# Casting loads head by head for v and the tails of batches 0 to 2, and another order of the first three tiles, in a fused attention and ReGLU kernel

## The chip, the cores and the metric

The kernel runs on one core of one Trainium2 chip. A core has a matrix engine (TensorE, PE in the profile; its weight loads are listed apart as PEld), a vector engine (VectorE, DVE), a scalar engine (ScalarE, ACT), GpSimd (POOL) and a synchronising engine (SyncE, SP), which here only issues DMAs. The on-chip memories are SBUF and PSUM; PSUM has eight banks, and PE writes only there. The metric is the device time of one launch in microseconds (us); the kernel's time is the median over its runs.

## The reference

Eight batches of eight heads, 576 positions, 64 values a head, in f32. Attention is causal by blocks of 64: a position sees its own block and all before it. The result, 4608 tokens of 512 values, goes through a ReGLU feed-forward of width 1536.

```python
scores = scale * np.matmul(q, k.transpose(0, 1, 3, 2))
scores = np.where(block_i >= block_j, scores, -1e9)
attn = exp(scores - max); attn = attn / (sum + 1e-9)
x = matmul(attn, v) laid out as 4608 x 512
out = (maximum(x @ w_gate, 0) * (x @ w_val)) @ w_out
```

## The kernel before

**Tiles.** The kernel computes in bf16 with f32 sums. The feed-forward runs over nine tiles of 512 tokens: tiles 0 to 7 hold the first 512 positions ("mains") of batches 0 to 7, tile 8 the last 64 positions ("tails") of all batches. Tile j needs the attention of batch j, transposed to `xT`. So attention of batch j+1 is woven into the feed-forward of tile j, and tile 0 stands behind a head that does the attention of batch 0 with no feed-forward beside it.

**Places.** A generator `ffn_gen` emits the feed-forward product by product. Everything else is an *act*, a named piece of work, with a *place* in the table `AT`: the number of products that come before it. A tile has 144 places in `AT`: 96 of gate and value products (L1095), 48 of output products (L1199 in tiles 0 and 1; from tile 2 on the output products are 42 pairs, L793, and the places are scaled). Tile 1 begins at place 144, tile 2 at 288, tile 3 at 432. Acts are emitted in the order of their places, and the order in which each engine works is the order of emission. An engine thus stands at an instruction whose input is late, and all that is emitted behind it on this engine waits. SP and POOL run ahead of PE's places as far as data and buffers allow. A product's result on PE goes to one of three PSUM banks `ffnp`, is relued by ACT (L1105, gate) and multiplied by DVE (L1115, value) into `hT`; the bank is then free.

**Acts of a round.** A round r is one pair of heads of batch r // 4. `s` computes its scores (PE, L454) and the first exps (ACT), `e` the last exp, `c` zeroes the masked corners, `a` and `b` multiply by v for the two heads (PE, L589) and normalise (DVE, into `xnat`), and `x` transposes into `xT`: rounds 4 to 7 on PE, from round 8 on by a DMA transpose from SP's queue (L638). Tails of batches 0 to 2 have acts of their own: `S`, `E`, `L` (scores, exps, last keys), `A` and `B` (products with v). From batch 3 on the tails are part of the rounds.

**Getting q, k and v in.** For batches 0 to 2, SP loads f32 into buffers `stage` (ten of 128 x 1024, in rotation), and an engine casts to bf16:

- q and k (`E1q0`, `E1q4`, `E1q6`, `E2q0`, `E2q4`): each partition gets four neighbouring positions of a head, 1 KB in one piece. Casts: `q0`, `k0`, `q4`, `q6`, and inside `q2`, `q24`.
- v: batch 1 head by head (L162, acts `E1v0`, `E1v4`, casts `ev0`, `ev4` on POOL, L223), batch 2 by chunks of 128 positions (`E2v0`, `E2v4`, L172, casts in `v2` on POOL, L231). Pieces of 256 B.
- tails of q, k and v (`T0`, `T1`, `T2`, L184), cast by `tc` on POOL (L209, L210, L217) and `td` on DVE.

The mains of batch 1 are then transposed on PE, one pair of heads at a time (`m0` to `m3`, L272, evicted by ACT and DVE, L281). Those of batch 2 are transposed by DMA into `perm` (L245, from `q2` and `q24`), and `u0` to `u3` bring them into order (L256).

From batch 3 on, POOL issues *casting loads* (L341): DMAs that read f32 from HBM and write bf16 to SBUF, with pieces of 256 B read and 128 B written. `l3` loads q and k of batch 3, `lv3` its v, `l4` and `lv4` those of batch 4. They need no stage and no cast. `dq3`, `d3`, `d4` are the DMA transposes behind them on SP (L350). `behind` in `load_qkv` is an instruction that the first load of a group waits for; `products[-1]` is the last gated product of DVE that has been emitted.

Weights come through `stage` too: `cg..`, `cv..`, `cw..` are the casts of pieces of the gate, value and output weights (L386); `w00` to `w21` load the output weights. `W0` to `W5` are sums of output weights on POOL (L698, L699). `o0` to `o3` store tile 0's output. `HOW` gives the engine of each act.

Of the kernel before, what the change touches and what calls it, by code (L numbers as in the profile page):

```python
# [11 lines left out]
BF = mybir.dt.bfloat16  # L12
# [5 lines left out]
def kernel(  # L18
# [10 lines left out]
    nc = tc.nc  # L29
# [94 lines left out]
    class Early:  # L124
# [33 lines left out]

        def load_v(self, h0, n):
# [127 lines left out]

        def pe_tails(self, evac):
# [14 lines left out]
    products = []  # L303
# [785 lines left out]
    def ffn_gen():  # L1089
        for j in range(B + 1):  # L1090
# [3 lines left out]
            def product(to, t, c, f):  # L1094
                nc.tensor.matmul(  # L1095
# [5 lines left out]
                )  # L1101

# [95 lines left out]
            def out_mm(op, s, f, n0, n1):  # L1198
                nc.tensor.matmul(  # L1199
# [5 lines left out]
                )  # L1205

# [61 lines left out]
    with tc.manual_schedule(engines={E.PE, E.DVE, E.Activation, E.Pool, E.SP}):  # L1268

        e0, e1, e2 = [Early(b) for b in range(3)]  # L1270
        w = {}
# [46 lines left out]
        def v_2():  # L1318
            e2.cast_v_chunks(0, pool)
            e2.cast_v_chunks(1, pool)  # L1320

# [3 lines left out]
        def mains_2(h0):  # L1325
            e2.cast_qk(h0, 4, (pool, pool))
            e2.transpose(h0 // 4)

        def load_tails(e):
            e.load_tails((0, 1))  # L1330
            e.load_tails((2,))
# [18 lines left out]

        def mains_1(hp):
            engs, banks = HOW[f"m{hp}"]
            if banks == "one":
                both = bank("one", BF)
                two = [both[:, 512 * t : 512 * t + 512] for t in range(2)]
            else:
                two = [bank(w, BF)[:, 0:512] for w in banks]
            e1.pe_mains(hp, [by[e] for e in engs], two)
# [88 lines left out]
            "E1v0": 32.16,  # L1447
# [3 lines left out]
            "E1v4": 32.19,  # L1451
            "T0": 32.19,
            "E2q0": 32.19,
            "T1": 32.23,
# [9 lines left out]
            "ev0": 32.33,  # L1464
# [3 lines left out]
            "ev4": 34.05,  # L1468
            "tc0": 34.05,
            "q2": 37.71,  # L1470
            "tc1": 48.64,
# [5 lines left out]
            "E2v0": 109.09,  # L1477
# [9 lines left out]
            "E2v4": 125.35,  # L1487
            "T2": 126.26,
# [17 lines left out]
            "td0": 156.81,  # L1506
            "t0": 163.43,
            "td1": 164.5,
# [10 lines left out]
            "v2": 191.07,  # L1519
# [10 lines left out]
            "tc2": 214.11,  # L1530
            "td2": 214.72,
# [66 lines left out]
            "m0": (("act", "dve"), "one"),  # L1598
            "m1": (("dve", "act"), ("sc", "ffn")),
            "m2": (("act", "act"), ("sc", "ffn")),  # L1600
            "m3": (("act", "act"), "one"),
# [41 lines left out]
        }  # L1643
        STEADY = {"s": 2, "e": 8, "c": 15, "a": 22, "b": 26, "x": 26.1}
# [49 lines left out]
            "E1q0": lambda: e1.load_qk(0, 4),  # L1694
            "E1q4": lambda: e1.load_qk(4, 2),
            "E1q6": lambda: e1.load_qk(6, 2),
            "E1v0": lambda: e1.load_v(0, 4),
            "E1v4": lambda: e1.load_v(4, 4),
            "T0": lambda: load_tails(e0),
            "T1": lambda: load_tails(e1),  # L1700
            "T2": lambda: load_tails(e2),
            "E2q0": lambda: e2.load_qk(0, 4),
            "E2q4": lambda: e2.load_qk(4, 4),
            "E2v0": lambda: e2.load_v_chunks(0),
            "E2v4": lambda: e2.load_v_chunks(1),
            "q0": lambda: e1.cast_qk(0, 4, (pool, None)),
            "k0": lambda: e1.cast_qk(0, 4, (None, by[HOW["k0"]])),
            "q4": lambda: e1.cast_qk(4, 2, [by[e] for e in HOW["q4"]]),
            "q6": lambda: e1.cast_qk(6, 2, [by[e] for e in HOW["q6"]]),
            "ev0": lambda: e1.cast_v(0, 4, pool),  # L1710
            "ev4": lambda: e1.cast_v(4, 4, pool),
            **{f"tc{b}": lambda e=e: e.cast_tails(True, 0, pool) for b, e in enumerate((e0, e1, e2))},
            **{f"td{b}": lambda e=e: e.cast_tails(False, 1, dve) for b, e in enumerate((e0, e1, e2))},
            **{f"m{hp}": lambda hp=hp: mains_1(hp) for hp in range(4)},
            "q2": lambda: mains_2(0),
            "q24": lambda: mains_2(4),
# [4 lines left out]
            "v2": v_2,  # L1721
# [7 lines left out]
            "lv4": lambda: load_qkv(4, (2,)),  # L1729
# [31 lines left out]
        for c in range(6):  # L1761
# [5 lines left out]
                "q2": 39.35,  # L1767
                "E2q4": 45.78,
                "s4": 94.33,
                "e4": 116.37,  # L1770
                "c4": 118.9,
                "e5": 119.89,
                "a4": 122.44,
                "b4": 122.71,
                "m2": 124.37,
                "c5": 124.58,
                "E2v4": 125.26,
                "a5": 126.96,
                "s6": 128.29,
                "b5": 128.47,  # L1780
                "e6": 128.55,
                "c6": 131.71,
                "x5": 133.24,
                "m3": 134.04,
                "x4": 137.38,
                "s7": 140.84,
                "b6": 140.91,
                "a6": 141.21,
                "e7": 142.62,
                "T2": 142.71,  # L1790
                "x6": 146.04,
                "c7": 147.83,
                "a7": 148.88,
                "b7": 149.16,
# [138 lines left out]
```

## Time and profile before

| what | value |
|---|---|
| time, median of 3 runs | 355.68 us (354.7, 355.68, 359.37) |
| the profiled execution's own time | 359.0 us |
| its span, first to last instruction | 357.1 us |
| mean granted clock of TensorE | 0.992 |
| PE / DVE / ACT / POOL busy | 96% / 60% / 55% / 47% |
| DMA | 155496 packets, 50.04 MB, 140 GB/s on average |
| the chain that ended last, by engine | PE 87%, DMA 4%, ACT 3%, DVE 3%, issue 1% |

The span is what the views of the trace divide up; the time of the launch lies some 1.9 us above it. A row of a timeline gives the start in us from the span's beginning, the length, the engine, the line of the kernel and the operation, with the tile that is written left of the arrow and those that are read right of it; in brackets stands how long the engine was idle before it, and who ended that. A row of a group gives the count, the busy time, the mean in ns of one, and after the bar the idle time in front of them. SPq and POOLq are the queues that issue DMAs. In a table by stage the busy times of the engines stand one after the other.

### The profile page before, as it was taken

How to read it: one execution, taken by the hardware profiler on the slowest of the kernel's cores; microseconds unless marked ns; L12 is line 12 of the kernel's file. 1: busy time of each engine (PE TensorE's matmuls, PEld its weight loads, DVE VectorE, ACT ScalarE, POOL GpSimd, SP SyncE). 2: the span in 40 equal slices, each digit the busy share in tenths (PEclk: the TensorE clock that was granted, in tenths of full speed). 3: DMA queues.
4: the chain of work that ended last, by engine and by line, in shares of the span. 5: the costliest groups of instructions: out<-in, count | busy, mean ns of one | idle time of the engine just before them, and what ended most of it. 6: DMA issues, size and time to landing. Idle time of an engine off the chain costs nothing.

```text
span 357.1 us, 8396 instructions
## 1 busy us (share of the span) xinstructions
PE 341.5 (96%) x3276; PEld 217.2 (61%) x3317; DVE 214.9 (60%) x552; ACT 196.8 (55%) x319; POOL 167.6 (47%) x199
## 2 busy tenths in 40 slices
PE   7889999999979999999999999999999999999994
PEld 3544455555534458555775567555855588888883
DVE  4654455667517566366636664567446657786783
ACT  4932756578322874555556553666266636735731
POOL 4647556579912930194009506980292042620630
PEclk9999999999998999999999999999999999999998
DMA  8999989999991999499739993999511013003005
GB/s 245 292 356 375 319 202 221 244 157 179 183 187 35 136 171 143 144 123 123 141 110 125 128 164 110 94 138 140 128 61 29 17 24 118 2 3 117 2 1 119
DMA packets 155496, 50.04 MB, mean 140 GB/s; under 512 B 134464, under 2 KB 151872, under 8 KB 155456
## 3 DMA queue, kind: packets, MB, share of 16 engines
q0 software_dynamic: 70480, 8.85, 47.5%
q1 hardware_dynamic: 79040, 33.96, 45.1%
q10 hardware_dynamic: 5936, 6.69, 5.8%
q8 instruction: 26, 0.43, 0.6%
q14 instruction: 14, 0.11, 0.1%
HBM read 37.75 MB, written 9.44 MB: 132 GB/s over the span
## 4 chain that ended last, share of the span: by engine, by line
PE 87%; DMA 4%; ACT 3%; DVE 3%; issue 1%; SPq 0%; POOL 0%; POOLq 0%; DVEq 0%
PE ffnp L1095 38%; PE ffnp L793 12%; PE upa L965 6%; PE one L793 5%; PE ffnp L1199 4%; PE sc L454 3%; PE upc L965 3%; PE ffnp L589 2%; DMA stage<-in_moe_w_gate_dram 2%; PE one L454 2%; DMA xT<-xnat 2%; ACT attnT L418 2%; PE ffnp L965 1%; PE one L589 1%; PE one L1095 1%
## 5 line engine op out<-in xcount | busy, mean ns | idle before, releaser
L1115 DVE TENSOR_TENSOR hT<-gate_sb,ffnp 128x512 bf16<-128x512 bf16 x82 | 56.1, 684 | 66.7 <-PE ffnp L1095 35.5
L1095 PE MATMUL ffnp<-xT,wg 128*128 128x512 bf16 x300 | 85.5, 383 | 4.4 <-DMA xT<-xnat 2.3
L1095 PE MATMUL ffnp<-xT,wv 128*128 128x512 bf16 x311 | 88.1, 382 | 1.4 <-issue 0.8
L1105 ACT ACTIVATE gate_sb<-ffnp 128x512 bf16<-128x512 f32 x79 | 48.0, 610 | 49.9 <-PE ffnp L1095 48.1
L459 ACT ACTIVATE attnT<-sc 128x1024 bf16<-128x1024 f32 x56 | 57.9, 1046 | 0.0
L1095 PEld LDWEIGHTS <-wg 128*128 128x128 bf16 x336 | 30.9, 98 | 36.5 <-issue 7.0
L1095 PEld LDWEIGHTS <-wv 128*128 128x128 bf16 x336 | 30.4, 98 | 33.8 <-issue 4.2
L341 POOL DMA_DIRECT2D q_bf<-in_q_dram x20 | 18.0, 913 | 53.2 <-DVE hT L1115 37.9
L825 ACT COPY ob<-ffnp 128x512 f32<-128x512 f32 x21 | 12.3, 585 | 43.7 <-PE ffnp L793 42.2
L793 PEld LDWEIGHTS <-stage 128*128 128x128 bf16 x336 | 32.5, 98 | 3.7
L589 PEld LDWEIGHTS <-attnT 128*128 128x128 bf16 x640 | 26.7, 98 | 12.6 <-issue 1.5
L793 PEld LDWEIGHTS <-hT 128*128 128x128 bf16 x252 | 24.1, 98 | 4.2 <-DVE hT L997 0.7
L341 POOL DMA_DIRECT2D v_bf<-in_v_dram x30 | 24.2, 857 | 1.5 <-DMA k_bf<-in_k_dram 0.9
L466 ACT ACTIVATE attnT<-one 128x512 bf16<-128x512 f32 (+1 forms) x28 | 15.1, 538 | 16.4 <-PE ffnp L454 15.5
L1199 PE MATMUL ffnp<-wo,hT 128*128 128x512 bf16 x89 | 22.2, 379 | 0.2
L454 PEld LDWEIGHTS <-kTm 64*128 64x128 bf16 x384 | 13.2, 94 | 14.2 <-issue 8.4
L793 PE MATMUL ffnp<-stage 128*128 128x256 bf16 x168 | 21.6, 273 | 0.0
L793 PE MATMUL ffnp<-wo,hT 128*128 128x256 bf16 x168 | 21.3, 273 | 0.1
L341 POOL DMA_DIRECT2D k_bf<-in_k_dram x20 | 18.0, 944 | 0.0
L454 PE MATMUL sc<-qTm,kTm 64*128 64x512 bf16 (+1 forms) x168 | 17.9, 305 | 0.0
L750 DVE TENSOR_TENSOR stage<-hT 128x512 bf16<-128x512 bf16 (+1 forms) x45 | 17.6, 394 | 0.5
L1001 POOL TENSOR_TENSOR hT<-attnT,gate_sb 128x512 bf16<-128x512 f32 x4 | 4.6, 1159 | 25.1 <-ACT gate_sb L1009 25.1
(185 smaller groups left out, 618.8 us busy)
## 6 DMA issues: line engine op xcount, KB each, us to landing
out_dram<-ob ACTq DMA_DIRECT2D x24, 256.0 KB, 2.3
stage<-in_moe_w_val_dram SPq DMA_DIRECT2D x6, 512.0 KB, 8.6
stage<-in_moe_w_gate_dram SPq DMA_DIRECT2D x6, 512.0 KB, 8.9
stage<-in_moe_w_out_dram SPq DMA_DIRECT2D x6, 512.0 KB, 10.5
q_bf<-in_q_dram POOLq DMA_DIRECT2D x20, 128.0 KB, 4.4
k_bf<-in_k_dram POOLq DMA_DIRECT2D x20, 128.0 KB, 6.0
v_bf<-in_v_dram POOLq DMA_DIRECT2D x20, 128.0 KB, 6.1
stage<-in_v_dram SPq DMA_DIRECT2D x19, 128.0 KB, 5.7
```

What stands on the lines that cost most here:

```text
L341: ins = nc.gpsimd.dma_start(dst, part_of)
L454: nc.tensor.matmul(o, kTm[b % 2][head_of(hh), c, hp, :], qT, start=True, stop=True)
L459: return lambda: nc.scalar.activation(at[:, :, lo : lo + 512], sc, AF.Exp, scale=scale)
L466: nc.scalar.activation(at[:, hh, 1024 : 1024 + w], third[hh][:, 0:w], AF.Exp, scale=scale)
L589: nc.tensor.matmul(av[:, p, :], at[:, col : col + 128], v_bf[b % 2][:, c, h, :], start=(p == 0), stop=(c == p), skip_group_check=True,)
L750: ins = (eng or nc.vector).tensor_tensor(out=s(i), in0=a, in1=b, op=op)
L793: nc.tensor.matmul(to, sums.of(c)[which]()[:, 128 * p : 128 * p + 128], right, start=first, stop=(c == 5), skip_group_check=True,)
L965: nc.tensor.matmul(to[:, 256 * f : 256 * f + 256], left(which, u // 2)[:, kc, lo : lo + 128], right[which](kc), start=new and (f, kc) == ( ...
L1095: nc.tensor.matmul(to, (wg, wv)[t][f // 4][:, c, 128 * (f % 4) : 128 * (f % 4) + 128], x[:, c], start=(c == 0), stop=(c == 3),)
L1105: nc.scalar.activation(gate_sb, gate, AF.Relu)
L1115: nc.vector.tensor_tensor(out=h, in0=gate_sb, in1=val, op=AX.mult)
L1199: nc.tensor.matmul(op, hT[f][:, 128 * s : 128 * (s + 1)], wo[f // 4][:, f % 4, n0:n1], start=(f == 0), stop=(f == 11),)
```

## The change

Five things change.

1. v of batches 1 and 2, and the tails of q, k and v of batches 0 to 2, are loaded by casting loads from POOL, two heads an act (`E1v0` to `E1v3`, `E2v0` to `E2v3`), with acts for the tails (`E1v4`, `E0v`, `E2v4` for v, `T0` to `T2` for q and k). The casts `ev0`, `ev4`, `v2`, `tc` and `td` are gone. The first load of each act waits for the last gated product that was emitted before it.
2. q and k of batch 1's second half are loaded four heads at a time (`load_wide`), and each is one cast instead of two. The loads wait for the last product of PE emitted before them (`marks`), except `E1q0`.
3. The transposes of batch 1 on PE are made for two pairs of heads at a time into two whole banks (`pe_wide` in `m0` and `m2`), and evicted pair by pair (`evac_wide`).
4. `l3`, `lv3` and `lv4` also wait for the last gated product.
5. The places of acts in tiles 0 to 2, and the engines of some casts and copies, are others.

```diff
+        def load_wide(self, hg, ts, tied=True):
+            behind = marks[-1] if tied and marks else None
+            for t in ts:
+                st = self.st[t, 4 * hg] = new_stage(1024)
+                ins = nc.sync.dma_start(
+                    st.rearrange("p (h n) -> p h n", h=4),
+                    (q, k)[t][self.b, 4 * hg : 4 * hg + 4, 0:512, :].rearrange(
+                        "h (p j) d -> p h (j d)", j=4
+                    ),
+                )
+                after(ins, behind)
+                behind = None
...
+        def casting_loads(self, pieces):
+            behind = products[-1] if products else None
+            for dst, src in pieces:
+                after(nc.gpsimd.dma_start(dst, src), behind)
+                behind = None
...
+        def load_v_casting(self, hp):
+            self.casting_loads(
+                [
+                    (
+                        v_bf[self.b % 2][:, 0:4, h, 0:64],
+                        v[self.b, h, 0:512, :].rearrange("(c p) d -> p c d", p=128),
+                    )
+                    for h in (2 * hp, 2 * hp + 1)
+                ]
+            )
...
+        def pe_wide(self, hg, two):
+            for t in range(2):
+                src = self.half(t, hg)
+                for i in range(8):
+                    nc.tensor.transpose(
+                        two[t][:, 128 * i : 128 * i + 128],
+                        src[:, i % 4, 128 * (i // 4) : 128 * (i // 4) + 128],
+                        ident,
+                    )
...
+                marks[:] = [ins]
...
+        def mains_2(hg):
+            for t in range(2):
+                e2.cast_wide(hg, t, pool)
+            e2.transpose(hg)
...
-            "l3": lambda: load_qkv(3, (0, 1)),
+            "l3": lambda: load_qkv(3, (0, 1), products[-1]),
...
-            "lv3": lambda: load_qkv(3, (2,)),
+            "lv3": lambda: load_qkv(3, (2,), products[-1]),
```

`load_v_tails` and `load_qk_tails` do the same for the last 64 positions: two loads for v, one for q and two for k, each of 512 pieces for q and 256 for the others.

The diff sets places in several layers; the net result for the acts that the text speaks of (a dash: there is no such act):

| act | place before | place after | act | place before | place after |
|---|---|---|---|---|---|
| `E1q0` | 20.29 | 31.89 | `u0` | 190.06 | 175.71 |
| `E1v0` | 32.16 | 32.25 | `E2v1` | - | 177.64 |
| `E2q4` | 45.78 | 32.32 | `u2` | 208.80 | 178.42 |
| `E1v1` | - | 32.65 | `E2v0` | 109.09 | 181.56 |
| `q4` | 32.36 | 33.06 | `E2v3` | - | 183.06 |
| `q6` | 32.36 | 44.94 | `u1` | 186.30 | 189.62 |
| `E1v2` | - | 81.55 | `E2v2` | - | 197.17 |
| `E1v3`, `E1v4` | -, 32.19 | 95.0 | `l3` | 218.57 | 206.37 |
| `T1` | 32.23 | 95.13 | `E2v4` | 125.26 | 233.2 |
| `e4` | 116.37 | 95.19 | `b10` | 257.52 | 254.65 |
| `T0` | 32.19 | 113.05 | `a11`, `b11` | 255.82, 255.91 | 256.06, 256.15 |
| `o0` | 211.88 | 121.41 | `x9` | 257.80 | 257.80 |
| `E0v` | - | 122.63 | `x10` | 258.51 | 265.03 |
| `m2`, `m3` | 124.37, 134.04 | 123.01, 126.7 | `x11` | 256.77 | 269.13 |
| `a5` | 126.96 | 129.46 | `lv3` | 267.98 | 299.67 |
| `E2q0` | 32.19 | 131.52 | `l4` | 319.56 | 319.14 |
| `q2`, `q24` | 39.35, 191.07 | 133.73, 137.09 | `a12` | 344.19 | 340.47 |
| `W0` | 224.67 | 165.0 | `d4` | 341.28 | 362.52 |
| `T2` | 142.71 | 169.39 | `x13` | 360.22 | 366.57 |

Engines: `cg00/01` and `cv00/23` go from DVE to ACT, `cg00/23` and `cv10` from POOL to ACT, `cv00/01` from DVE to POOL, `cv20` from POOL to DVE, `cw21/1` from DVE to ACT. The second half of `u0` goes from POOL to ACT, the first half of `u2` from DVE to ACT, the second half of `u1` from DVE to POOL.

More of the change, by code (lines that the diff above doesn't have):

```diff
@@ L1349, in piece @@
             return lambda: cast_w(w[n], by[HOW.get("c" + name, "pool")], rows)
+        wide = {}
         def mains_1(hp):
             engs, banks = HOW[f"m{hp}"]
[L1353 to L1358, printed above, removed]
+            hg = hp // 2
+            if hp % 2 == 0:
+                wide[hg] = [bank(n, BF) for n in banks]
+                e1.pe_wide(hg, wide[hg])
+            e1.evac_wide(hp, wide[hg], [by[n] for n in engs])
         AT = {
@@ L1446 @@
             "w10": 32.12,
-            "E1v0": 32.16,
+            "E1v0": 16.06,
+            "E1v1": 32.25,
+            "E1v2": 32.26,
+            "E1v3": 32.27,
             "w21": 32.16,
@@ L1486 @@
             "c5": 124.67,
-            "E2v4": 125.35,
-            "T2": 126.26,
+            "E2v4": 180,
+            "T2": 164,
             "a5": 127.05,
@@ L1885 @@
                 "e16": 440.19,
+                "L4": 440.2,
                 "c16": 446.75,
+            }
+        )
+        AT.update(
+            {
+                "E1q0": 7.94,
+                "E1v1": 30.9,
+                "w01": 31.9,
+                "w00": 32.05,
+                "E1v0": 32.28,
+                "E1v2": 32.29,
+                "E2q0": 32.29,
+                "E1v4": 32.32,
+                "q4": 33.06,
+                "q6": 39.6,
+                "cv20": 39.67,
+                "E0v": 59.28,
+                "q2": 83.63,
+                "m0": 83.76,
+                "e4": 114.3,
+                "T0": 116.1,
+                "c4": 119.55,
+                "b4": 122.07,
+                "c5": 122.64,
+                "a4": 122.93,
+                "m2": 123.01,
+                "m3": 126.7,
+                "a5": 129.46,
+                "b5": 130.09,
+                "s7": 136.5,
+                "c6": 137.1,
+                "a6": 140.99,
+                "x6": 149.0,
+                "x7": 152.75,
+                "T2": 167.67,
+                "E0": 168.68,
+                "A0": 176.07,
+                "E1": 194.84,
+                "t2": 215.84,
+                "E2v4": 233.82,
+            }
+        )
```

458 lines of the change are left out of this document (317 added, 141 removed).

## The prediction

> **What bounds the kernel now.** I read the page's engine totals first, then the 40 slices, then busy time by stage, then who made TensorE (PE) wait.
>
> ```profile
> span 357.1 us, 8396 instructions
> PE 341.5 (96%) x3276; PEld 217.2 (61%) x3317; DVE 214.9 (60%) x552; ACT 196.8 (55%) x319; POOL 167.6 (47%) x199
> ...
> PEclk9999999999998999999999999999999999999998
> GB/s 245 292 356 375 319 202 221 244 157 179 183 187 35 136 171 143 144 123 123 141 110 125 128 164 110 94 138 140 128 61 29 17 24 118 2 3 117 2 1 119
> q0 software_dynamic: 70480, 8.85, 47.5%
> ```
>
> PE is busy in 341.5 of 357.1 us and no other engine passes 60%. The change leaves PE's work as it is: 32 transposes of 128x128 for batch 1 stay 32, and no product is added or dropped. It can therefore only act through the 357.1 - 341.5 = 15.6 us in which PE stands still, and through its clock. The stages show where those lie (columns: window; length; busy time and count of PE, PEld, DVE, ACT, POOL; PE clock; DMA share; GB/s):
>
> ```profile
> 0.00:10.00 10.00, 7.32 (x42) 3.27 (x42) 4.50 (x14) 5.34 (x7) 4.88 (x20) 1.00 0.87 252
> 10.00:20.00 10.00, 8.45 (x131) 5.60 (x129) 7.70 (x23) 7.41 (x11) 5.22 (x11) 1.00 1.16 303
> 20.00:30.00 10.00, 9.04 (x45) 4.06 (x45) 4.12 (x9) 4.58 (x8) 5.82 (x6) 1.00 1.08 366
> 50.00:60.00 10.00, 9.84 (x113) 5.68 (x115) 5.40 (x19) 9.10 (x16) 4.62 (x7) 1.00 0.94 215
> 100.00:110.00 10.00, 7.69 (x38) 3.25 (x38) 2.56 (x5) 2.61 (x4) 0.00 (x0) 0.83 1.13 169
> 320.00:358.00 38.00, 32.26 (x291) 27.97 (x288) 24.93 (x47) 17.00 (x31) 10.21 (x9) 0.96 0.20 56
> ```
>
> The first 30 us lose 2.7 + 1.6 + 1.0 = 5.2 us while the first weights arrive, and the end loses 5. Between them one stage stands out, 100 to 110 us: 2.3 us idle, and a granted clock of 0.83, which is half speed for 3.4 us, another 1.7 us. Together **4.0 us are lost at the step from tile 1 to tile 2**. The timeline of PE and of SP's queue, then the chain that ended last, name the cause:
>
> ```profile
> 102.79 0.38 PE L1095 MATMUL ffnp<-xT,wg 128*128 128x512 bf16 x1
> 104.58 0.38 PE L1095 MATMUL ffnp<-xT,wg 128*128 128x512 bf16 x1 [1.29 <-DMA xT<-xnat]
> 105.92 1.01 PE L1095 MATMUL ffnp<-xT,wg 128*128 128x512 bf16 x2 [0.96 <-DMA xT<-xnat]
> ...
> 88.95 4.70 SPq L350 DMA_TRANSPOSE qTm<-q_bf  x1
> 96.00 4.65 SPq L638 DMA_TRANSPOSE xT<-xnat  x3
> ...
> 98.07 1.26 SPq L638
> ...
> 99.43 6.44 DMA xT<-xnat
> ...
> 92.96 4.83 POOL L341 DMA_DIRECT2D v_bf<-in_v_dram  x6
> ```
>
> Tile 2 needs four DMA transposes (`x8` to `x11`). Three were queued together at 96.00: `x11` came first, waited for the last values of its round, and so held back `x9`, whose round (`a9`, `b9`, places 231 to 233) was over. The last, `x10`, took 6.44 us to land, while the six casting loads of `lv3`, issued from 92.96, shared the DMA engines.
>
> **The change part by part.** *Tile 1 to tile 2.* `lv3` goes from place 267.98 to 299.67, behind a product of tile 2, and the transposes are queued `x9`, `x10`, `x11`. `x9` can go when the transpose of 88.95 leaves SP at 93.65, 4.4 us before its old slot of 98.07. `x11` waits for the same values as before and is issued at about 96.3, since `x10` (`b10` now ahead of `a11`) goes before it. At the old 6.44 us it lands at 102.7; PE needs it as fourth product, some 0.65 us after 102.6. I count a remainder of 0.3 us: **-3.7 us**, bounds 0 (the crowd is only replaced by another) and -4.0.
>
> By the Trainium skill, "TensorE: Matmul & The Clock Gate", § What's actually happening, the clock falls for a window of about 3.4 us that runs freely from execution to execution, so that one idle stretch may or may not cost it. The row of 0.83 agrees with one such window; by the rule the 1.7 us would be absent in some runs.
>
> *Loads of v and the tails.* These rows price what moves from SP's queue and POOL's casts to POOL's casting loads:
>
> ```profile
> L341 POOL DMA_DIRECT2D v_bf<-in_v_dram x30 | 24.2, 857 | 1.5 <-DMA k_bf<-in_k_dram 0.9 <-issue 0.3
> L341 POOL DMA_DIRECT2D q_bt<-in_q_dram x5 | 4.0, 790 | 0.0
> L341 POOL DMA_DIRECT2D k_bt<-in_k_dram x10 | 6.6, 699 | 0.0
> L198 POOL CAST q_bf<-stage 128x1024 bf16<-128x1024 f32 x3 | 3.3, 1096 | 1.7 <-DVE recip L526 1.2 <-DMA stage<-in_q_dram 0.5
> 55.10 0.61 POOL L209 CAST q_bt<-stage 64x512 bf16<-64x512 f32 x1
> 55.66 0.39 POOL L210 CAST k_bt<-stage 64x256 bf16<-64x256 f32 x1
> 56.28 0.41 POOL L217 CAST v_bf<-stage 64x256 bf16<-64x256 f32 x1 [0.23 <-DMA stage<-in_v_dram]
> DMA to landing us min/median/max: 4.6/6.9/9.6
> ```
>
> (The last row is the landing of v_bf's loads.) A head's load has 512 pieces of 256 B, as a q_bt load has: about 0.75 us of POOL. There are 16 of those (12.0 us), 6 tails of v at about 0.70 (4.2), 3 of q at 0.79 and 6 of k at 0.70 (6.6): **22.8 us added to POOL**. Gone are four casts of v of the size of that q_bf cast (4.4) and three sets of tails at 0.61 + 0.39 + 0.41 (4.2), and DVE loses its `td` casts. POOL is busy 47%, so the sum is no cost by itself. What counts is when three things in its order come due.
>
> ```profile
> 35.06 1.22 POOL L198 CAST q_bf<-stage 128x1024 bf16<-128x1024 f32 x1 [0.28 <-DMA stage<-in_q_dram]
> 39.27 2.03 POOL L386 CAST wo<-stage 128x1024 bf16<-128x1024 f32 x2 [2.99 <-DMA stage<-in_moe_w_out_dram]
> 41.98 3.92 POOL L386 CAST wo<-stage 128x1024 bf16<-128x1024 f32 x4 [0.68 <-DMA stage<-in_moe_w_out_dram]
> ...
> 42.76 5.13 PE L1199 MATMUL ffnp<-wo,hT 128*128 128x512 bf16 x22
> ...
> 50.17 0.39 PE L272 MATMUL sc<-ident,q_bf 128*128 128x128 bf16 x4
> ...
> 52.62 0.48 PE L589 MATMUL ffnp<-v_bf,attnT 128*128 128x65 bf16 x10
> ```
>
> First, the casts of `wo`. They wait for DMA (2.99, 0.68 us), and the GB/s slices from 27 to 36 us stand at 375, the highest of the page. `E1v0` was behind these weights on SP's queue; now POOL issues its 1024 pieces at about 36.3, ahead of their landing and on another queue. A packet of POOL's queue takes 47.5% x 357.1 x 16 / 70480 = 38 ns of one engine, so 1024 take 2.5 us of all 16; by bytes, 0.26 MB at 375 GB/s, 0.7 us. I take 1.4 us for the last weights. Their casts end at 45.9, and PE, which began the output products at 42.76, uses the third group of `wo` 16 to 19 products later, each 5.13 / 22 = 0.23 us, so at 46.4 to 47.1: a slack of about 0.8. So **+0.6 us**, bounds 0 and 1.7.
>
> Second, the batch 1 casts `q4`, `q6` (two at 1.1) come behind the issues of `E1v1` (1.5): 45.9 + 1.5 + 2.2 = 49.6, and `m2`, its transposes at 50.17 before, stands some two products earlier, at about 49.7. `a5` needs `E1v1`: issued until 47.4, landed 4.6 to 6.9 later, 52.0 to 54.3, against about 52.9 (place 129, just behind the row of 52.62). Both move with the first stall. **+0.5 us**, bounds 0 and 2.5.
>
> Third, after those stand 14 more loads (`E1v2`, `E1v3`, `E1v4`, `T1`, `T0`, `E0v`: 3.0 + 1.4 + 2.2 + 2.2 + 1.4 = 10.2), then four casts for batch 2 (4.3): 49.6 + 10.2 + 4.3 = 64.1. The transposes behind them on SP take 1.4 to issue and 3.5 to 5.2 to land:
>
> ```profile
> perm<-q_bf SPq DMA_TRANSPOSE x1, 5.2
> perm<-k_bf SPq DMA_TRANSPOSE x1, 3.5
> 58.95 1.46 SPq L245 DMA_TRANSPOSE perm<-q_bf  x1
> ...
> 69.47 0.81 PE L1095 MATMUL ffnp<-xT,wg 128*128 128x512 bf16 x3
> ...
> 121.71 1.03 PE L1095 MATMUL ffnp<-xT,wv 128*128 128x512 bf16 x4
> ...
> 76.77 3.77 POOL L341 DMA_DIRECT2D q_bf<-in_q_dram  x4
> ...
> 18.26 0.59 PE L1095 MATMUL ffnp<-xT,wg 128*128 128x512 bf16 x2 [0.31 <-DVE xT L633]
> ```
>
> They are there at 69 to 70.7; `u0` and `u2`, which move up to places 175 and 178 and in half to ACT, come due at about 69.3 and 69.9 (a place is one product of the feed-forward; the row of 69.47 holds places 176 to 178). ACT and DVE queue the relus and gated products of tile 1 behind them, and PE has three banks in hand. I count 0, bounds 0 and 5.
>
> *Later.* `lv3` now starts when tile 2's first gated product is done, about 105.5 without the bubble, takes 4.83 to issue and up to 6.9 to land: 117.2. `a12`, at place 340 (the row of 121.71), comes due at 121.7 - 4.0 = 117.7. **+0.2**, bounds 0 and 2.2 (landing 9.6). `l3` starts at 76.77 before; now `T2` (due at about 69), two copies of the `u` acts at about 1.1 and eight loads of v stand ahead: 69 + 2.2 + 2.2 + 6.0 = 79.4; its q lands by about 88.7, when SP reaches its transpose anyway: 0.
>
> *The head.* Casts of the first weights change engines: `cg00/01` to ACT is ready some 0.5 us later, and the product after it was waiting for xT until 18.26 anyway. The order on SP up to the output weights is unchanged. 0, bounds -0.6 and +0.6, one cast of 512 values (0.61 in the q_bt row). The exps (`e4` up by 21 places) relieve ACT in 50 to 60 us, 9.10 busy, where PE idles 0.16: at most that.
>
> By the Trainium skill, "SBUF — State Buffer", § SBUF: two separate sides, a DVE copy from SBUF to SBUF can keep POOL from writing descriptors, and a load of 620 ns took 3100 there. The row of 857 ns over 30 issues shows nothing of the sort here, though no row shows the loads beside such a copy alone. By the rule, loads that meet a `u` copy of DVE would be held for its length, which would count for the third rival below.
>
> Sum: -3.7 + 0.6 + 0.5 + 0.2 = **-2.4 us**, on the profiled execution's 359.0: 356.6. That execution is 3.3 above the median of 355.68, and the runs are 354.7, 355.68 and 359.37: it is like the slowest. The spread, 4.7, is about the size of the loss at tile 2, so the faster runs may have lost less there. If they lost nothing, the change gives 355.68 + 1.3 = 357.0; if as much, 355.68 - 2.4 = 353.3. I take the middle, **355.1 us**.
>
> **The rivals.** *Nothing is added.* The stalls at 43 to 55 us don't come, because queues share better than I reckon, and the bubble closes: 355.68 - 4.0 = 351.7. For it: each of those stalls hangs on less than 1.5 us. Over 2%, under 348.6, would need 3 us more, out of the head.
>
> *The bubble stays.* `l3` ends later, and `E2v4` now lies behind it on POOL, so other casting loads crowd the transposes: the 4.0 us stay and the additions come on top, 359.0 + 1.3 = 360.3, or 357.0 by the median. Against it: `x9` gains 4.4 us in the queue.
>
> *POOL's line runs late* (the slower side). A casting load can wait for an earlier one to land, as the 0.9 us behind k_bf in the first price row shows. If such waits space the issues at 1.2 us (an estimate: the longest landing, 9.6, over eight loads in flight) instead of 0.75, the 16 loads from 45.9 end 7.2 us later. With a slack near 0 at `u0` and `u2`, ACT and DVE stand there, PE's three banks cover about 1 us, and a clock window adds 1.7: 7.2 - 1 + 1.7 = +7.9, so 356.6 + 7.9 = 364.5. It decides from about 1.1 us per issue. For it: landings up to 9.6 us in such trains. Against: the 30 issues averaged 0.86 with twice the pieces.
>
> **How the numbers follow.** Forecast 0.55 (353.3 to 357.0); nothing added 0.16 (349 to 353); bubble stays 0.18 (357 to 361); POOL late 0.11 (361 to 368). The range runs from 351 to 361.5: half of the second case and most of the fourth are left out, under 2 in 10. Two per cent, 7.1 us, is about what a measurement of this kernel can tell from no change. Faster 0.03, within 0.88, slower 0.09.
>
> **What would show it.** In the changed profile: the stage of tile 2's start with PE at 9.8 of 10 and clock 1.00, and `x9` before `x10` and `x11` on SP; waits of PE for `wo`, v_bf or batch 1's transposes of 0.5 to 2 us between 43 and 55; POOL's casts for batch 2 done by about 64; no wait of ACT or DVE for perm; PE still near 341.5 busy. I am wrong if PE's busy time falls, if the perm waits exceed 2 us, or if the transposes of tile 2 still land after its start.

## The result, and the profile after

The changed kernel takes **353.22 us** (median of 19 runs, 352.54 to 356.04), beside 356.6 (354.7 to 361.98, 19 runs) for the kernel before on the same chip: a ratio of 0.9928, 95% interval [0.9904, 0.9952]. In a later comparison, beside other kernels, it took 352.66 against 356.29: 0.9924 [0.9889, 0.9958]. The ratios leave out runs that lie more than 1.5% above the fastest of their kernel, of which only the kernel before has any here, while medians and ranges count every run. So it is faster by 0.5 to 1% and within the 2% that had been called no change. The forecast of 355.1 was 1.9 us too high. As a gain, 0.6 us had been forecast (355.68 to 355.1) and 3.4 were measured (356.6 to 353.22).

The page of the changed kernel, its totals, PE's clock in slices, and the queue of POOL's DMAs:

```profile
span 351.5 us, 8431 instructions
PE 341.3 (97%) x3317; PEld 216.4 (62%) x3317; DVE 210.5 (60%) x541; ACT 201.8 (57%) x326; POOL 176.6 (50%) x213
...
PEclk9999999999999999999999999999999999999999
...
q0 software_dynamic: 83776, 10.49, 58.0%
```

PE is as busy as before (341.3 us), POOL 9 us more, and its queue now has 58.0% instead of 47.5%. What shrank is PE's idle time, from 15.6 to 10.2 us, and the granted clock is 0.99 to 1.00 in every stage. (The trace of before holds 41 matmuls fewer than weight loads, 3276 and 3317; about 2 of its 15.6 us are holes under 0.1 us, which may be matmuls that were not recorded.) Two stages of the changed kernel, and the longer one of the kernel before:

```profile
60.00:100.00 40.00, 40.00 (x451) 21.23 (x449) 22.58 (x58) 25.98 (x40) 31.00 (x41) 1.00 1.39 138
100.00:110.00 10.00, 10.00 (x95) 5.10 (x94) 6.37 (x19) 3.58 (x6) 4.83 (x6) 1.00 1.04 144
```

```profile
60.00:100.00 40.00, 39.10 (x455) 21.32 (x462) 26.21 (x67) 22.66 (x38) 32.76 (x42) 1.00 1.51 186
```

The 4.0 us at tile 2's start are gone, and so is 0.9 us between 60 and 100, of which the prediction had not spoken; in before's trace it lies in holes of at most 0.15 us each. To place the gain, I compared the start of PE's weight load for each product in both traces. Up to place 12 the changed kernel is 0.4 us ahead, at place 288 1.4, at place 300 5.7, and this stays to the end. From place 288 to 300 the kernel before takes 7.75 us and the changed one 3.50. The two executions lie 5.75 us apart (359.0 and 353.25); the medians only 3.4, because the profiled execution of before lay 2.4 us above the median of these 19 runs.

The boundary in the changed kernel, first PE's timeline:

```profile
101.38 0.38 PE L1193 MATMUL ffnp<-xT,wg 128*128 128x512 bf16 x1
101.71 0.81 PE L1193 MATMUL ffnp<-xT,wg 128*128 128x512 bf16 x3
```

Then SP's queue, and the row for `xT` in the table of DMAs issued from 92 to 99 us (count, median us to landing):

```profile
93.06 4.43 SPq L736 DMA_TRANSPOSE xT<-xnat  x3
```

```profile
xT<-xnat SPq DMA_TRANSPOSE x3, 4.1
```

`x9` leaves SP at 93.06 instead of 98.07, and the three transposes land 4.1 us after their issue. PE runs on without a gap.

POOL's line through tiles 0 and 1, with the points that the prediction had timed:

```profile
35.82 1.69 POOL L183 DMA_DIRECT2D v_bf<-in_v_dram  x2
38.89 2.02 POOL L484 CAST wo<-stage 128x1024 bf16<-128x1024 f32 x2 [1.38 <-DMA stage<-in_moe_w_out_dram]
41.74 3.01 POOL L484 CAST wo<-stage 128x1024 bf16<-128x1024 f32 x3 [0.82 <-DMA stage<-in_moe_w_out_dram]
44.98 0.61 POOL L484 CAST wo<-stage 128x512 bf16<-128x512 f32 x1 [0.22 <-DMA stage<-in_moe_w_out_dram]
...
48.42 1.04 POOL L174 CAST k_bf<-stage 128x1024 bf16<-128x1024 f32 x1 [0.36 <-DMA stage<-in_k_dram]
49.40 4.20 POOL L183 DMA_DIRECT2D v_bf<-in_v_dram  x6
...
62.10 1.04 POOL L174 CAST k_bf<-stage 128x1024 bf16<-128x1024 f32 x1
...
104.71 4.83 POOL L439 DMA_DIRECT2D v_bf<-in_v_dram  x6 [10.11 <-DVE stage L802]
```

The casts of `wo` end at 45.59 (45.90 before), `q6` at 49.46 (forecast 49.6), the casts for batch 2 at 63.14 (forecast 64.1), and `lv3` starts at 104.71 (forecast 105.5). An issue cost 0.70 us on average in the train at 49.40 (four loads of 512 pieces and two of 256), and none of them waited.

### The profile page after: what moved, and what is told of

It reads as the page before. It is cut to its first block, busy times and chain, and to the rows that moved or that the text cites. A ratio compares the mean times of both kernels' runs of the same rounds, so it can differ in the third digit from the quotient of the medians.

```text
span 351.5 us, 8431 instructions
## 1 busy us (share of the span) xinstructions
PE 341.3 (97%) x3317; PEld 216.4 (62%) x3317; DVE 210.5 (60%) x541; ACT 201.8 (57%) x326; POOL 176.6 (50%) x213
## 4 chain that ended last, share of the span: by engine, by line
PE 91%; DMA 3%; ACT 2%; DVE 2%; issue 1%; SPq 0%; POOL 0%; POOLq 0%; DVEq 0%
PE ffnp L1193 40%; PE ffnp L891 11%; PE ffnp L1298 6%; PE upa L1063 6%; PE one L891 5%; PE sc L552 3%; PE upc L1063 3%; PE ffnp L687 2%; PE one L552 2%; DMA stage<-in_moe_w_gate_dram 2%; ACT attnT L516 2%; PE one L687 2%; PE ffnp L1063 1%; PE one L1193 1%; PE sc L687 1%; PE ffnp L649 1%
## 5 line engine op out<-in xcount | busy, mean ns | idle before, releaser
L1193 PE MATMUL ffnp<-xT,wv 128*128 128x512 bf16 x328 | 90.0, 379 | 0.0
L1193 PE MATMUL ffnp<-xT,wg 128*128 128x512 bf16 x316 | 86.6, 379 | 1.2 <-ACT wg L484 0.5
L1298 PE MATMUL ffnp<-wo,hT 128*128 128x512 bf16 x96 | 23.5, 379 | 0.0
```

The source lines that it names most:

```text
L1193: ins = nc.tensor.matmul(to, (wg, wv)[t][f // 4][:, c, 128 * (f % 4) : 128 * (f % 4) + 128], x[:, c], start=(c == 0), stop=(c == 3),)
L1298: ins = nc.tensor.matmul(op, hT[f][:, 128 * s : 128 * (s + 1)], wo[f // 4][:, f % 4, n0:n1], start=(f == 0), stop=(f == 11),)
```

## The experiments

Theories. **Crowd**: `lv3`'s six loads slow the landing of tile 2's transposes. **Order**: `x11` ahead of `x9` on SP is what makes them late. Rival: the casting loads themselves bring or cost something. The other kernels ask what slack POOL's line, the output weights and the head have. "Before" is the kernel before on the same chip: 356.01 for the first four, 356.46 for the next four, 356.29 for the last four.

| kernel | median, us | ratio to before, 95% |
|---|---|---|
| `lv3` late, in the kernel before | 354.49 | 0.9947 [0.9926, 0.9968] |
| order of transposes, in the kernel before | 356.09 | 1.0012 [0.9971, 1.0053] |
| both, in the kernel before | 354.54 | 0.9970 [0.9945, 0.9995] |
| change with `lv3` early | 355.12 | 0.9976 [0.9948, 1.0003] |
| change, POOL held 5 us | 356.96 | 1.0053 [1.0011, 1.0094] |
| change, POOL held 11 us | 364.03 | 1.0253 [1.0200, 1.0306] |
| change, `E1v1` ahead too | 353.00 | 0.9934 [0.9909, 0.9958] |
| change, v of batches 1, 2 by SP | 359.96 | 1.0162 [1.0090, 1.0233] |
| change, v of batch 2 by SP | 358.17 | 1.0052 [1.0022, 1.0083] |
| change, other head | 354.29 | 0.9972 [0.9940, 1.0004] |
| change, other head and `E1v1` ahead | 353.76 | 0.9966 [0.9931, 1.0001] |
| the change again | 352.66 | 0.9924 [0.9889, 0.9958] |

**1. Crowd or order.** Four kernels: each edit alone in the kernel before, both, and the changed kernel with `lv3` put back.

```diff
-            "lv3": lambda: load_qkv(3, (2,)),
+            "lv3": lambda: load_qkv(3, (2,), products[-1]),
...
+        AT.update({'lv3': 299.67})
```

> The kernel before, with only lv3 (six casting loads of batch 3's v) moved from place 267.98 to 299.67, behind the first product of tile 2. If the crowd of casting loads is what made the transposes of tile 2 late: the last of them lands in about 4.7 us instead of 6.44, the stage of tile 2's start loses under 1 us, and the time falls by 2 to 4 us. If the order on SP's queue is the cause (x11 ahead of x9): the three transposes still leave SP together at about 96 to 100.7, PE still idles 1 to 2 us there, and the time falls by 1 us at most.

```diff
+        AT.update({'b10': 254.65, 'x9': 257.8, 'x10': 265.03, 'x11': 269.13})
```

> The kernel before, with only the transposes of tile 2 queued x9, x10, x11 and b10 ahead of a11; lv3 stays at 267.98. If the order is the cause: x9 leaves SP at about 93, the last transpose lands ahead of tile 2's first product or at most 0.5 us behind it, and the time falls by 2 to 4 us. If the crowd is the cause: the six casting loads still lie beside x10 and x11, whose landing stays near 6.4 us, PE still waits about 1 us or more, and the time falls by 1 us at most.

Both edits together, and the reverse of the first one in the changed kernel:

> The kernel before with both edits and nothing else of the change (no casting loads for batches 1 and 2, no tails). If the whole gain of the change lies at the step from tile 1 to tile 2: the same ratio as the change, 0.990 to 0.995, about 353.5 us, and the stage of tile 2's start with PE at 10.0 of 10. If the casting loads of v and the tails themselves bring part of it: at least 1 us slower than the change.

> The changed kernel with only lv3 put back to place 267.98 and its wait for tile 2's first product taken away. If the crowd is the cause: the loss at the step to tile 2 comes back, 2 to 4 us, and the time is that of before, about 356. If the order is: at most 1 us slower than the change, with x9 still at about 93 on SP.

Measured: moving `lv3` alone takes 1.5 us off the median, the order alone nothing (+0.1), both no more than `lv3` alone, and putting `lv3` back into the changed kernel costs 1.9 to 2.5. The landing of the transposes, from the tables of DMAs issued around 90 to 101 us (count, KB each, median us to landing): with `lv3` moved; with the order alone; in the kernel before; in the changed kernel with `lv3` early:

```profile
xT<-xnat SPq DMA_TRANSPOSE x3, 4.0
```

```profile
v_bf<-in_v_dram POOLq DMA_DIRECT2D x4, 128.0 KB, 6.0
...
xT<-xnat SPq DMA_TRANSPOSE x3, 6.5
```

```profile
xT<-xnat SPq DMA_TRANSPOSE x3, 6.5
```

```profile
xT<-xnat SPq DMA_TRANSPOSE x3, 7.0
```

Whenever `lv3`'s loads lie beside them the transposes take 6.5 to 7.0 us, otherwise 3.4 to 4.1 (3.4 with both edits, 4.1 in the changed kernel), whatever their order. The crowd is the cause. It also widens the scatter: with `lv3` moved alone the nine runs lie between 353.54 and 354.92, with the order alone between 354.79 and 360.61, and those of before between 353.77 and 362.25. The profiled execution with the order alone (354.79) shows no gap at tile 2, and that with `lv3` early 0.8 us:

```profile
102.85 0.38 PE L1193 MATMUL ffnp<-xT,wg 128*128 128x512 bf16 x1 [0.81 <-DMA xT<-xnat]
```

So the 6.5 us decide nothing in some executions and 4 us in others, and the median gains less (1.5) than the trace of before suggested (4.0). The order isn't without effect in these traces: in both, the three transposes are queued from about 92 us instead of 96, which hides most of the longer landing. At the median it brought nothing.

**2. What the rest of the change brings.** The changed kernel once more, beside the last three.

> The changed kernel itself, beside the three that follow. If moving lv3 alone is the whole gain: within 0.5 us of what that move alone gave (354.49, a ratio of 0.9947). If the rest of the new order brings something too: about 1.2 us less, near 353.2, as in the stages from 60 to 90 us, where PE stood 0.4 to 0.6 us with lv3 moved alone and not at all in the changed kernel.

It gave 352.66, so 1.8 us less than with `lv3` moved alone. The ratios' intervals overlap, but the traces agree with a gain: the 144 places of tile 1 take 44.10 to 45.24 us in the four profiled executions with the old order (the kernel before and the first three) and 43.31 to 43.32 in six with the new order of tile 1 that hold nothing back. Two waits of PE with the old order, with `lv3` moved alone and with both edits:

```profile
62.30 0.59 PE L1095 MATMUL ffnp<-xT,wg 128*128 128x512 bf16 x2 [0.29 <-DVE xT L633]
```

```profile
63.59 0.59 PE L1095 MATMUL ffnp<-xT,wg 128*128 128x512 bf16 x2 [0.79 <-DVE xT L633]
```

There PE waits for DVE, and with the order alone 0.67 us at the same place. In the changed kernel DVE has 22.58 us of work between 60 and 100 us instead of 26.21 in the kernel before, and these waits are absent. They make up 0.3 to 0.8 of the 0.8 to 1.9 us; in before's own trace no wait of PE there is longer than 0.15 us, so that DVE as the cause is argued for the rest and not shown. Which of the moved acts does it was not taken apart.

**3. POOL's line.** Nine, then nineteen memsets of the zero tile between the casting loads of `E0v` and the casts for batch 2.

```diff
+        def held():
+            e0.load_v_tails()
+            for _ in range(9):
+                nc.gpsimd.memset(zeros, 0.0)
...
-            "E0v": e0.load_v_tails,
+            "E0v": held,
```

> The changed kernel with POOL kept busy for about 4.7 us more (nine memsets of the zero tile) between the casting loads of batch 0's tails and the casts for batch 2. This measures the slack of POOL's line, which the prediction put near 0 at u0 and u2. If the slack is near 0: the casts for batch 2 end at about 68 instead of 63.1, u0 and u2 wait about 4 us for perm, PE loses some 3 to 6 us and the time is about 356 to 359. If there is slack of 5 us or more: the same as the change within 0.7 us.

> As the kernel with nine memsets, with nineteen (about 10 us). If the slack is near 0: 8 to 11 us slower than the change. If it is about 5 us: 4 to 6 us slower. If the line can run 10 us late: the same as the change within 1 us. Whatever waits first (u0 and u2 for perm, l3's transposes for tile 2, batch 2's tails) shows in the waits.

POOL's timeline with nine memsets:

```profile
58.11 5.34 POOL L1789 MEMSET zeros<- 128x512 bf16 x9
...
66.34 1.03 POOL L174 CAST k_bf<-stage 128x1024 bf16<-128x1024 f32 x1
```

What waits behind it, in the timelines of ACT and DVE and then among PE's waits from 40 to 110 us (us in total, times, longest):

```profile
69.25 1.08 ACT L330 COPY kTm<-perm 128x512 bf16<-128x512 bf16 x1 [1.73 <-DMA perm<-k_bf]
72.25 1.05 ACT L330 COPY qTm<-perm 128x512 bf16<-128x512 bf16 x1 [1.91 <-DMA perm<-q_bf]
74.40 0.84 DVE L330 COPY kTm<-perm 128x512 bf16<-128x512 bf16 x1 [4.72 <-DMA perm<-k_bf]
```

```profile
PE ffnp L1193 <- ACT gate_sb L1204: 1.6, 1, 1.6
PE ffnp L1193 <- DVE hT L1214: 1.1, 1, 1.1
```

The casts for batch 2 end at 67.37, 4.2 us later than in the changed kernel; PE is 4.0 us behind at place 204, and the median rises by 3.7. The copies `u0` and `u2`, which ACT and DVE have ahead of relus and products, are where it shows. But PE stands only 2.8 of these microseconds. The rest is its clock, which the stages from 74 to 82 us give as 0.66 and 0.91 (4 x 0.34 + 4 x 0.09 = 1.7 us):

```profile
74.00:78.00 4.00, 2.87 (x21) 1.46 (x20) 2.75 (x4) 2.39 (x4) 4.00 (x5) 0.66 2.01 118
78.00:82.00 4.00, 4.00 (x31) 1.79 (x28) 1.29 (x3) 2.80 (x5) 1.34 (x3) 0.91 0.81 50
```

With nineteen, 11.2 us of memsets, the casts end 10.0 us later, PE stands 7.2 us and its clock is at 0.50 from 78 to 86 us; PE is 11.0 behind at place 204, and the median rises by 10.8. So POOL's line has a slack of some 2.5 us (5.3 - 2.8) before PE stands, or 4 (11.2 - 7.2) in the longer case, and the slower clock behind the stall takes most of that back. That each microsecond on POOL costs nearly one of the kernel is the sum of the two.

**4. Loads beside the output weights.**

```diff
+        AT.update({'E1v1': 32.251})
```

> The changed kernel with the second group of batch 1's casting loads of v (E1v1) moved ahead of the casts of the output weights too, so that 2048 pieces instead of 1024 are issued while those weights land. If the pieces share the DMA engines with the weights, as the prediction had it: the weights are 1 to 1.5 us later still, the casts of wo end at about 47 instead of 45.6, PE waits up to 1 us for them. If they wait behind the weights that are queued already: the wo casts end as in the change within 0.3 us, the loads land after 9 to 11 us, and the time is the same within 0.5 us.

POOL with two groups ahead:

```profile
35.51 3.18 POOL L183 DMA_DIRECT2D v_bf<-in_v_dram  x4
38.66 2.05 POOL L484 CAST wo<-stage 128x1024 bf16<-128x1024 f32 x2
41.43 3.01 POOL L484 CAST wo<-stage 128x1024 bf16<-128x1024 f32 x3 [0.72 <-DMA stage<-in_moe_w_out_dram]
44.67 0.61 POOL L484 CAST wo<-stage 128x512 bf16<-128x512 f32 x1 [0.23 <-DMA stage<-in_moe_w_out_dram]
```

The casts end at 45.28, as in the changed kernel with 1024 fewer pieces ahead (POOL's rows start 0.3 us earlier in this execution). The median is the same, as the second branch had it. But its reason, that the pieces wait behind the weights, holds only at first. The changed kernel's DMA queues between 37.5 and 39.9 us, when POOL had issued everything, and then from 43 to 45, with the last weights still landing:

```profile
q1 hardware_dynamic: 480, 0.93, 104.6%
...
v_bf<-in_v_dram POOLq DMA_DIRECT2D x1, 64.0 KB, 9.7
```

```profile
q1 hardware_dynamic: 475, 0.49, 88.1%
q0 software_dynamic: 478, 0.06, 45.5%
```

For 2.4 us POOL's queue (q0) moves no packet, while SP's (q1) keeps all engines busy. From about 40 us on both move, and from 43 to 45 they move packet for packet, with two groups too (475 of q0, 480 of q1). So the engines are shared. A second group only makes POOL's queue longer, not its share, and 1024 pieces last about as long as the weights do (until 45 us); the experiment can't tell what the first 1024 cost. The kernel of the next experiment with no casting load there can: the casts of `wo` end at 44.74, and at 45.17 in the kernel with nine memsets, which has one group ahead and whose PE is within 0.01 us of it from place 12 to place 96:

```profile
41.17 3.57 POOL L484 CAST wo<-stage 128x1024 bf16<-128x1024 f32 x4 [0.69 <-DMA stage<-in_moe_w_out_dram]
```

```profile
44.56 0.61 POOL L484 CAST wo<-stage 128x512 bf16<-128x512 f32 x1 [0.22 <-DMA stage<-in_moe_w_out_dram]
```

By these two traces the first group makes the last weights 0.4 us later, and PE waits for none of them. The second group's price falls on what comes next: its pieces land after 11.1 and 12.5 us (8.2 and 9.7 for the first group in the changed kernel), SP's load for `q6` takes 0.9 us longer to land and batch 2's two loads behind it 1.2 and 1.8, and PE waits 0.3 us for `q6`:

```profile
48.97 1.04 POOL L174 CAST k_bf<-stage 128x1024 bf16<-128x1024 f32 x1 [1.14 <-DMA stage<-in_k_dram]
```

**5. v by SP again.** Both batches, then batch 2 alone; the tails stay casting loads.

```diff
-            **{f"E2v{c}": lambda c=c: e2.load_v_casting(c) for c in range(4)},
+            "E2v0": lambda: e2.load_v_chunks(0),
+            "E2v1": lambda: e2.load_v_chunks(1),
+            "E2v2": lambda: e2.cast_v_chunks(0, pool),
+            "E2v3": lambda: e2.cast_v_chunks(1, pool),
...
+        AT.update({'E2v0': 109.09, 'E2v1': 125.35, 'E2v2': 181.56, 'E2v3': 183.06})
```

> The changed kernel with v of batches 1 and 2 loaded by SP and cast by POOL as in the kernel before; the tails stay casting loads and the places stay those of the change. If the loads of v by themselves change nothing, and the gain is that of the step to tile 2: the same as the change within 1 us. If SP's queue, which these loads left, is what made the room for the transposes of tile 2: x9 leaves SP later than 93, PE waits there again and the time is 2 to 4 us longer. If the casting loads cost something in tile 1: up to 1 us faster than the change.

> The changed kernel with only batch 2's v loaded by SP and cast by POOL (the places of before); batch 1's v stays with the casting loads. Undoing both batches cost 6.7 us. If that came from batch 1, whose SP loads and casts left POOL standing at 52 to 57 us: the same as the change within 0.7 us, batch 2's q and k casts done by about 64 and no wait of PE near 65 to 72. If it came from batch 2's loads on SP, ahead of batch 2's q and k there: 4 to 7 us longer than the change, with POOL's casts for batch 2 waiting for stage.

The edit shown is that of batch 2 alone. The first expectation missed in all its branches: 6.7 to 7.3 us longer with both batches. In the second, 5.5 us with batch 2 alone is in the range of the branch that blames batch 2's loads, but POOL's casts for batch 2 wait for PE there and not for `stage`. The timelines of SP and of POOL with batch 2 alone:

```profile
42.63 11.17 SPq L246 DMA_DIRECT2D stage<-in_v_dram  x4
...
56.49 1.03 SPq L164 DMA_DIRECT2D stage<-in_k_dram  x1
```

```profile
56.00 0.61 POOL L183 DMA_DIRECT2D k_bt<-in_k_dram  x1 [1.40 <-DMA v_bf<-in_v_dram]
...
63.67 1.04 POOL L174 CAST q_bf<-stage 128x1024 bf16<-128x1024 f32 x1 [2.26 <-PE sc L1193]
...
67.47 1.04 POOL L174 CAST k_bf<-stage 128x1024 bf16<-128x1024 f32 x1
```

The four loads of v hold SP for 11.17 us and put the last load of batch 2's second half at 57.5 instead of 54.6; POOL's casting loads beside them land after 7.1 us (median of the four of v issued from 48.99) instead of 3.6, POOL stands 3.1 us on such landings (1.40, 0.81 and 0.86), and its casts for batch 2 end at 68.51 instead of 63.14. PE is then 3.7 us behind at place 204; it also waits 1.5 us for `q_bt` and 1.1 for `v_bf`. (That profiled execution, 362.16, is 4 us above its median for another gap, at tile 3's start; these rows lie ahead of it.) With both batches the casts end at 69.61 and PE is 5.5 us behind. So it is POOL's line again that runs late, as in the third experiment, here by issues that wait for earlier landings. The finding has a limit: these loads stood ahead of batch 2's last q and k on SP (places 109 and 125, `E2q0` at 131.5), where the kernel before had them behind. Loads by SP at a later place were not tried. With both batches POOL also stood 4.77 us ahead of the tails of v for a reason that the trace doesn't name; this stays open.

**6. The head.** The first of gate's casts back to POOL, two of ACT's casts exchanged.

```diff
+                "cg00/01": "pool",
...
+        AT.update({'cv00/23': 4.103, 'cg01/23': 4.104})
```

> The changed kernel with the first casts of the weights as in the kernel before (the first of gate's casts on POOL again) and ACT's next two casts of weights in the other order. If the first 23 us lose what ACT's queue there makes them lose (0.4 to 0.5 us of waits on ACT): 0.4 to 0.9 us less than the change, about 352.6. If xT is what comes last there, as the prediction reckoned for this place: the same within 0.3 us.

> The kernel with the changed head and batch 1's second group of casting loads ahead of the casts of the output weights as well. Either alone is worth 0.2 to 0.9 us at most, so 352.3 to 353.0; the same as the one with two groups ahead (353.0) if the head gives nothing.

Neither came: 354.29 and 353.76, 1.6 and 1.1 us longer than the change. In the trace of the first, PE is 0.5 us ahead at place 12 and 0.5 behind at place 144. One row lies between:

```profile
52.90 0.46 PE L687 MATMUL ffnp<-v_bf,attnT 128*128 128x65 bf16 x10 [0.68 <-DMA v_bf<-in_v_dram]
```

That is `a5`. PE was there 0.2 us earlier than in the changed kernel (52.22 and 52.40), and the loads of v took 6.9 us to land instead of 6.2. How much of this is the changed head is open: the profiled executions with the changed kernel's head reach place 12 at 21.8 to 22.2 us, so 0.4 us there is scatter. The rest of the loss isn't in that trace (353.68, span 351.8). In the second kernel PE waits 0.82 us for `q6`, as with two groups ahead. The profiled execution of the second, at 357.9, shows where such a loss can be, at tile 3's start:

```profile
142.67 0.38 PE L1193 MATMUL ffnp<-xT,wg 128*128 128x512 bf16 x1 [0.61 <-DMA xT<-xnat]
144.85 0.59 PE L1193 MATMUL ffnp<-xT,wg 128*128 128x512 bf16 x1 [1.80 <-DMA xT<-xnat]
```

It is the gap of tile 2, one tile later: the three transposes that SP issues for it from 134 us on land after 6.0 us there and after 3.4 in the changed kernel. Why a changed head should bring it more often stays open.

## Why the prediction was right, and where it was wrong

**Tile 1 to tile 2** (-3.7): right in size and place, -4.25 against the same trace. The mechanism was only half right. The step gave the gain to two things at once, `x9`'s earlier slot and `lv3`'s move; the medians give all of it to `lv3`. It is worth 1.5 us in the kernel before and 1.9 to 2.5 in the changed one. That faster runs may have lost less there, as the prediction said, is what the runs show. On "The bubble stays" (0.18): the casting loads of `E2v4` did not take `lv3`'s place as a crowd; the landing fell from 6.5 to 4.1 us. The lost clock was read rightly: in before's trace the granted clock is 0.50 from 106.0 to 109.0 us, and 0.93 and 0.66 in the half microseconds on either side, so half speed for 3.4 us. By the Trainium skill, "TensorE: Matmul & The Clock Gate", § What's actually happening, the slow clock comes with a freely running window of about this length. The traces agree: with `lv3` early, PE idles 0.8 us at the same place and the clock stays at 1.00 from 96 to 112 us.

**The output weights** (+0.6): wrong, 0. That POOL's 1024 pieces take engine time from weights queued ahead of them on SP is right. The failed step is the size: 1.4 us for the last weights, against a slack of 0.8. They came 0.4 us later, so PE didn't wait. What the step left out is that POOL's queue moved nothing until about 40 us, 2.4 us after its last issue. The Trainium skill, "DMA: Bandwidth & Descriptors", § Queues, rings and completion order, has each engine take turns between its queue rows, packet by packet. The rows from 43 to 45 us agree (478 packets and 475). Why none moved before 40 us no view shows: the pieces can have been late into their queue or late out of it.

**Batch 1's casts and `a5`** (+0.5): 0. The cast ended at 49.46 where I had 49.6, but the stall hung on the first one, which didn't come, and `a5`'s v landed in time. That it is close, the kernel with the other head showed: there PE waits 0.68 us.

**POOL's line** (0, bounds 0 and 5): right in the changed kernel. The casts were 1.0 us ahead of the reckoned time, and no copy waited for perm. The rival "POOL's line runs late" had the mechanism right, ACT and DVE standing at `u0` and `u2` and a slow clock behind the stall; what it lacked was its condition. It decides from about 1.1 us per issue, and the issues took 0.70 to 0.85. Landings of 7 us, beside SP's loads of v, did make issues wait. Its argument against, that 30 issues averaged 0.86 us "with twice the pieces", is misread: 20 of them have 1024 pieces and 10 have 256, so 1.5 times on average. On the rule of the Trainium skill, "SBUF — State Buffer", § SBUF: two separate sides, that DVE's copies can hold up POOL's descriptors (the page names f32 copies for it; these are bf16), the six loads issued beside DVE's `u` copies took this:

```profile
70.10 0.64 DVE L330 COPY kTm<-perm 128x512 bf16<-128x512 bf16 x1
72.34 1.25 DVE L330 COPY qTm<-perm 128x512 bf16<-128x512 bf16 x1
...
70.15 4.61 POOL L183 DMA_DIRECT2D v_bf<-in_v_dram  x6
```

At 0.77 us each for 512 pieces (0.85 for the two at 35.82, without such a copy beside them), and landing after 3.9 us (median), nothing like a held load is seen.

**`lv3` for `a12`, `l3`** (+0.2 and 0): both 0, `lv3` 0.8 us earlier than reckoned.

**The head** (0, within 0.6): no effect shown. The changed kernel is 0.4 us ahead at place 12 in the two profiled executions, but place 12 is reached at 21.80 to 22.21 us in eight traces with its head and at 21.80 to 22.81 in the four with the old one.

**Left out: tile 1.** The prediction priced the new order of tile 1 at nothing or a loss, and the relief of ACT at 0.16 at most. It gave 0.8 to 1.9 us in the traces. The failed step is that I looked for PE's idle time only in stages where it was large; the 0.9 us between 60 and 100 us were not looked at. In part PE waited there for DVE, which the change relieves of casts and copies.

Together, at the medians: the forecast of 0.6 us of gain was made of 1.9 at the step to tile 2 (half of 3.7) less 1.3 of additions. Measured were 1.5 for `lv3`, no additions, and some 1.8 more from the rest of the change, the 3.4 us. That the number came within 1.9 us all the same is partly luck: the median of before was 355.68 in the three runs of the forecast and 356.6 in nineteen, which hides 0.9 us of the difference. The result lies on the border between the forecast's own range (353.3 to 357.0) and that of "Nothing is added" (349 to 353), and of the two the latter describes better what happened: the bubble closed and no stall took its place. It has no term for tile 1 either.

## What to carry to other kernels

When a DMA that the next stage waits for has no slack, look at what other queues send in the same microseconds: here six loads on another engine's queue turned a landing of 4.0 us into 6.5 and the time into a scatter of 8 us, while reordering the waiting queue by itself brought nothing at the median. Before moving work to an engine that is half idle, measure the slack of its queue at the first thing that depends on it: POOL was busy 50%, and 5.3 us more work at one place cost the kernel 3.7. A single trace is one draw from a scatter; take the size of a stall that comes and goes from many runs, not from the row.

## What the runs showed of the hardware that was not expected

Two casting loads issued by POOL while SP's large weight loads were queued moved no packet for 2.4 us after their issue, then one packet for each of SP's (478 and 475 from 43 to 45 us), and landed after 8.2 and 9.7 us; the last weights came 0.4 us later. Six casting loads, landing after 6.0 to 7.3 us themselves, slowed three DMA transposes beside them from 4.0 to between 6.5 and 7.0 us. SP took 11.17 us, between 42 and 54, to issue four loads of v of 1024 pieces, 2.7 ns a piece, where POOL issued six casting loads in 4.20 us at 49.40, four of 512 pieces and two of 256, 1.6 ns a piece. After a stall of PE of 2.8 us the granted clock cost another 1.7 us.
